# Block 0 by two half-size transposing DMAs, weight loads held back until the first loads have landed, and first projections of 256 columns

## The chip, the cores and the metric

The kernel runs on one core of a Trainium2 chip. Five engines work at once, each from an instruction queue of its own and in order: TensorE (PE in the profile, its weight loads shown as PEld), VectorE (DVE), ScalarE (ACT), GpSimd (POOL) and SyncE (SP). They wait for one another on semaphores. Transfers between the device memory and the on-chip memory are issued by SP and ACT and carried out by 16 DMA engines that both share. The metric is the device time of one launch in microseconds (us), as the median of several runs.

## The reference

The input `A_x` is one sequence of 2048 tokens with 512 features, in bfloat16. Two branches are computed from it and mixed by a gate:

```python
x = A_x                                            # (1, 2048, 512)
g = sigmoid((x * gate_w).sum(-1, keepdims=True))
# A: dilated local attention, 32 heads of 16, window 8, dilation 2
q, k, v = split(x @ wqkv)                          # wqkv (512, 1536)
logits[s, w] = q[s] . k[s - 2w] * 16**-0.5, masked where s - 2w < 0
a = (softmax(logits) weighted sum of v[s - 2w]) @ wo
# B: an MLP over the tokens, inner size 1792
h = layernorm(x)                                   # over the 512 features
b = transpose(gelu(h^T @ w1 + b1) @ w2 + b2)       # w1 (2048, 1792), w2 (1792, 2048)
return g * a + (1 - g) * b
```

All matrix products have bfloat16 operands and are summed in fp32.

## The kernel before

The kernel writes no instruction straight to an engine. It declares operations (`sch.add`, `sch.dma`, lines 89 to 124) with the names of the buffers that each reads and writes, an estimated duration, and extra dependencies: `deps` become real waits on semaphores, `after` only fixes an order. A planner (lines 126 to 232) then simulates the five queues with these estimates, and with 340 KB per us and 2 us of latency for transfers, and so settles the order of every queue before launch. On the chip each engine runs its list in that order and waits only for what an operation names.

What bears on the change is the beginning. The activations are wanted in two layouts: `X`, tokens on partitions (plain loads `ld_x`, four tiles of 128 tokens each), for the layer norm and the token MLP; and `XT`, features on partitions (transposing loads `ld_xt`), for the projections to q, k and v. `XT` comes in four blocks of 512 tokens, here called XT0 to XT3. The weights `wqkv` come as slices: q in two halves by the contraction (d0 and d1, then d2 and d3), here wq01 and wq23 of 256 KB each; all of k (wk, 512 KB); all of v (wv, 512 KB). The order of issue, lines 478 to 489, is

```python
ld_w(0, 0, 2, "act")   # wq01, the only load that ACT issues
ld_xt(0)               # all that follow are issued by SP, in this order
ld_w(0, 2, 2)          # wq23
ld_w(1, 0, 4)          # wk
ld_xt(1)
ld_x(0, 4); ld_x(4, 4); ld_xt(2); ld_xt(3); ld_x(8, 4); ld_x(12, 4); ld_w(2, 0, 4)
```

From the fifth load on, SP waits before an issue until the load five places earlier in the list `init_dmas` has landed (`throttle`, line 447).

While these loads are under way, PE multiplies zeros: nine matmuls of 512 columns (`warm1`, line 531). Then come the first projections (`pf_...`, lines 652 to 657): block 0 of q with d0 and d1 into four PSUM banks (8 matmuls of 512 columns), the same banks with d2 and d3 (8), and k of block 0 into the four other banks (16). ACT evicts each bank (`f_evq`). The list `seq_proj` follows: q and k of block 1, then of blocks 2 and 3, then v, and after that the gate (`emit_gz`), the first MLP product (line 848), the second (line 887), and the output projection (line 904). Between them lie short bursts of PE for the attention logits (`qkr`, line 693) that need products made by DVE (`qkm`, line 685); their place in PE's list is fixed by the planner. DVE begins with the layer norm's statistics (`ln1`, line 549) of the tiles that `ld_x(0, 4)` brings, and its order up to the softmax is written out by hand in `chain(...)`, lines 966 to 970.

Of the kernel before, what the change touches and what calls it, by code (L numbers as in the profile page):

```python
# [13 lines left out]
D = 512  # L14
# [321 lines left out]
def bass_gated_mix__sliding_local_dilated__mixer_token_mlp__prompt_kernel(nc, A_x, A_wqkv, A_wo, B_x, B_w1, B_b1, B_w2, B_b2, gate_w, out, dbg=None):  # L336
    with contextlib.ExitStack() as es:
        block = es.enter_context(nc.Block())
        view, pview, off, total = _views(nc, es)
        ps = es.enter_context(nc.psum_tensor("ps", [128, 8, 512], FP32))  # L340
        esem = {e: es.enter_context(nc.semaphore("sem_" + e)) for e in ("pool", "act", "dve", "pe")}
        sch = _Sched()

        x2d = A_x[0]
# [7 lines left out]
        XT = view("XT", BF16, [(S, 4), (1, S)])  # L352
# [68 lines left out]
        def sub(ap_, offs, dims):  # L421
            return bass.AP(ap_.tensor, ap_.offset + offs, [list(ap_.ap[0])] + [list(d) for d in dims])

        def psub(ap_, p0, np_, offs, dims):
            pst = ap_.ap[0][0]
            return bass.AP(ap_.tensor, ap_.offset + p0 * pst + offs, [[pst, np_]] + [list(d) for d in dims])

        A = sch.add
# [13 lines left out]
        def mk_dma(dst, src):  # L442
            return lambda e: e.dma_start(dst, src)

        init_dmas = []

        def throttle():
            return [init_dmas[-5]] if len(init_dmas) >= 5 else []

        def prev_dma():  # L450
            return [init_dmas[-1]] if init_dmas else []
# [9 lines left out]
        def ld_w(tn, d0, n, q="sp"):  # L461
            ds = sch.dsem("wqkv%d_%d" % (tn, d0))
            op = sch.dma(q, mk_dma(WQKV[:, d0:d0 + n, tn * D:(tn + 1) * D], wqkv_v[:, d0:d0 + n, tn * D:(tn + 1) * D]),
                         n * 128 * D * 2, ds, writes=["wqkv%d_%d" % (tn, dt) for dt in range(d0, d0 + n)],
                         deps=throttle() if q == "sp" and n == 4 else [], after=prev_dma() if q == "sp" else [],
                         issue=0.65 if n == 4 else 0.45, name="d_wp%d_%d" % (tn, d0))
            if q == "sp":
                init_dmas.append(op)
            return op

        def ld_xt(sb):
            ds = sch.dsem("xt%d" % sb)
            dst = XT[:, :, sb * 512:(sb + 1) * 512]
            op = sch.dma("sp", lambda e: e.dma_start_transpose(dst, x2d[sb * 512:(sb + 1) * 512, :]), 512 * D * 2, ds,
                         writes=["xt_%d" % t for t in range(4 * sb, 4 * sb + 4)], deps=throttle(), after=prev_dma(), name="d_xt%d" % sb)
            init_dmas.append(op)

        ld_w(0, 0, 2, "act")
        ld_xt(0)
        ld_w(0, 2, 2)  # L480
        ld_w(1, 0, 4)
        ld_xt(1)
        ld_x(0, 4)
        ld_x(4, 4)
        ld_xt(2)
        ld_xt(3)
        ld_x(8, 4)
# [4 lines left out]
                after=prev_dma(), name="d_gw", issue=0.3)  # L492
        sch.dma("sp", mk_dma(B1R, B_b1.rearrange("(t p) -> t p", p=128)), 4096, ds_b, writes=["b1r"], deps=throttle(),
                name="d_b1", issue=0.3)
        d_b2 = sch.dma("sp", mk_dma(B2R, B_b2.rearrange("(t p) -> t p", p=128)), 4096, ds_b, writes=["b2r"], deps=throttle(),
                       name="d_b2", issue=0.3)
# [16 lines left out]
        for g in range(4):  # L513
            d_wo = sch.dma("sp", mk_dma(psub(WO, 32 * g, 32, 0, [(D, 4), (1, D)]), wov[g]), 32 * 4 * D * 2, ds_wo,
                           writes=["wo%d" % g], deps=throttle(), name="d_wo%d" % g)
# [7 lines left out]
        def f_warm(n):  # L523
            def fn(e):
                ins = None
                for _ in range(n):
                    ins = e.matmul(ps[:, 7, :], lhsT=WARM[:, 0:128], rhs=WARM, start=True, stop=True)  # L527
                return ins
            return fn

        last_tx = A("pe", f_warm(9), 4.0, reads=["outs0"], writes=["lg7_0", "lg7_1"], name="warm1", prio=-100)

        ALLXT = ["xt_%d" % t for t in range(NST)]

# [11 lines left out]
        for hf in range(2):  # L546
            t0 = 8 * hf
            for t in range(t0, t0 + 8):
                A("dve", (lambda t_: (lambda e: e.bn_stats(out=ST6[:, t_, :], in_=X[:, t_, :])))(t), 0.59,  # L549
                  reads=["x%d" % t], writes=["st6_%d" % t], name="ln1_%d" % t, prio=0)  # L550
# [13 lines left out]
              reads=["zc%d" % hf], writes=["sd%d" % hf], name="ln_sqrt%d" % hf, prio=0)  # L564
            A("dve", (lambda t0_: (lambda e: e.reciprocal(out=cols(RSTD, t0_, 8), in_=cols(SD, t0_, 8))))(t0), 0.25,
              reads=["sd%d" % hf], writes=["rstd%d" % hf], name="ln_rstd%d" % hf, prio=0)
# [15 lines left out]
        last_main = [None]  # L582

        def main_bank():
            b = main_idx[0] % 4
            main_idx[0] += 1
            return b
# [40 lines left out]
            A("dve", lambda e: e.tensor_tensor(out=C2, in0=OMG, in1=B2C, op=ALU.mult), 0.15,  # L628
              reads=["omg", "b2c"], writes=["c2"], name="g_c2", prio=0)

        def f_proj(tn, dl, sb, bank, d0=0, d1=4):
            def fn(e):
                ins = None
                for dt in range(d0, d1):
                    lhsT = sub(WQKV, dt * 3 * D + tn * D + dl, [(4, 128)])
                    ins = e.matmul(ps[:, bank, :], lhsT=lhsT, rhs=XT[:, dt, sb * 512:(sb + 1) * 512],  # L636
                                   start=(dt == 0), stop=(dt == 3))
                return ins
            return fn

# [8 lines left out]
        tnames = ["q", "k", "v"]  # L649
        first = [(tn, dl) for tn in range(2) for dl in range(4)]  # L650
        fbn = [["acc%d" % b] for b in range(4)] + [["lg%d_0" % b, "lg%d_1" % b] for b in range(4, 8)]
        for (b0, d0, d1) in ((0, 0, 2), (0, 2, 4), (4, 0, 4)):
            for b in range(b0, b0 + 4):
                tn, dl = first[b]
                last_main[0] = A("pe", f_proj(tn, dl, 0, b, d0, d1), 0.216 * (d1 - d0),
                                 reads=ALLXT[0:4] + ["wqkv%d_%d" % (tn, dt) for dt in range(d0, d1)],
                                 writes=fbn[b], after=[last_main[0]], name="pf_%s%d_%d" % (tnames[tn], dl, d0))
        for b, (tn, dl) in enumerate(first):
            A("act", f_evq(tn, dl, 0, b), 0.52, reads=fbn[b] + (["k5pad"] if tn == 1 else []),
              writes=["%s5_%d_0" % (tnames[tn], dl)], name="ev_%s%d_0" % (tnames[tn], dl), prio=0)  # L660
# [7 lines left out]
        for (tn, dl, sb) in seq_proj:  # L668
            if (tn, dl, sb) == (2, 1, 0):
                emit_tb()  # L670
            xr = ALLXT[4 * sb:4 * sb + 4]
            bank = main_bank()
            last_main[0] = A("pe", f_proj(tn, dl, sb, bank), 0.866,
                             reads=xr + ["wqkv%d_%d" % (tn, dt) for dt in range(4)],
                             writes=["acc%d" % bank], after=[last_main[0]], name="pj_%s%d_%d" % (tnames[tn], dl, sb), prio=0)
            A("act", f_evq(tn, dl, sb, bank), 0.62, reads=["acc%d" % bank] + (["k5pad"] if tn == 1 else ["v5pad"] if tn == 2 else []),
              writes=["%s5_%d_%d" % (tnames[tn], dl, sb)], name="ev_%s%d_%d" % (tnames[tn], dl, sb), prio=0)
# [25 lines left out]
        for wh in range(2):  # L703
# [6 lines left out]
            for (dl, c0, nc_) in pieces:  # L710
# [3 lines left out]
                  reads=["q5_%d_%d" % (dl, sb) for sb in range(c0, c0 + nc_)] +  # L714
                        ["k5_%d_%d" % (dl, sb) for sb in range(max(c0 - 1, 0), c0 + nc_)] + ["k5pad"],
                  writes=wr, name="qkm_%d_%d_%d" % (wh, dl, c0), prio=0)
                if c0 + nc_ == 4 and dl % 2 == 1:
# [4 lines left out]
                    else:  # L722
                        for wl in range(4):
                            qop = A("pe", f_qkr(prs, (wl,)), 0.5, reads=rd, writes=["lg%d_0" % (4 + wl), "lg%d_1" % (4 + wl)],
                                    name="qkr_%d_%d_%d" % (wh, dl, wl), prio=-100 + wl, delay=BURST_DELAY)
                            A("act", (lambda wh_, wl_: (lambda e: e.activation(out=LGB[:, 4 * wh_ + wl_, :], in_=ps[:, 4 + wl_, :], func=AF.Copy)))(wh, wl),  # L726
                              0.55, reads=["lg%d_0" % (4 + wl), "lg%d_1" % (4 + wl)], writes=["lw%d" % (4 * wh + wl)],
                              name="lev_%d_%d" % (wh, wl), prio=0)
# [16 lines left out]
        def lw(hf):  # L745
            return ["lw%d" % w for w in range(4 * hf, 4 * hf + 4)]
# [6 lines left out]
        for hf in range(2):  # L753
# [3 lines left out]
              reads=["outs1"], writes=lw(hf), name="sm_sub%d" % hf, prio=0)  # L757
            if hf == 0:
                A("act", lambda e: e.activation(out=col(SD, 0), in_=col(ZC, 0), func=AF.Exp, scale=0.0), 1.5,
                  reads=["zc0"], writes=["sd0"], name="sm_pre")  # L760
            A("act", (lambda hf_: (lambda e: e.activation(out=ATT[:, 4 * hf_:4 * hf_ + 4, :], in_=LGB[:, 4 * hf_:4 * hf_ + 4, :],  # L761
                                                          func=AF.Exp)))(hf), 1.95,
              reads=lw(hf), writes=["att%d" % hf], name="sm_exp%d" % hf, prio=0)
# [10 lines left out]
        for hf in range(2):  # L774
# [3 lines left out]
              reads=["rs"], writes=["att%d" % hf], name="sm_nrm%d" % hf, prio=0)  # L778
# [3 lines left out]
        for c in range(4):  # L782
            for dh_hi in range(4):
                pst = V5.ap[0][0]
                src = bass.AP(V5.tensor, V5.offset + dh_hi * pst + 512 * c, [[4 * pst, 32], [KROW, 4], [1, VROW]])
                dst = psub(V3, 32 * c, 32, 4 * dh_hi * VSTR, [(VSTR, 4), (1, VROW)])
                v3_ops.append(sch.dma(V3Q, mk_dma(dst, src), 32 * 4 * VROW * 2, ds_v3, issue=(1.2 if V3Q == "pool" else 0.65),
                               reads=["v5_%d_%d" % (dl, sb) for dl in range(4) for sb in range(4)] + ["v5pad"],
                               writes=["v3_%d_%d" % (c, dh_hi)], deps=pb2_readers, name="d_v3_%d_%d" % (c, dh_hi)))
# [22 lines left out]
        for t in range(4):  # L812
            tb = []
            for wh in range(2):
# [3 lines left out]
                  writes=["pv%d_%d" % (buf, k_) for k_ in range(4)] + [qk_res, k_res, ["pb0_0", "pb0_1", "m4_0", "m4_1", "m2_0", "m2_1", "m1", "rs"]][buf],  # L818
                  name="avm_%d_%d" % (t, wh))
            b0, b1 = tb  # L820
            for (nm, o_, i_, n_, res) in (("ava", b0, b1, 4, None), ("avb", b0, b0, 2, 2), ("avc", b0, b0, 1, 1)):
# [4 lines left out]
                  writes=["pv%d_%d" % (o_, k_) for k_ in range(n_)], name="%s_%d" % (nm, t))  # L826
            if t < 3:
                ds_ot = sch.dsem("ot%d" % t)
                for c in range(4):
                    for g in range(4):  # L830
                        sch.dma("sp", mk_dma(psub(OT, 32 * g, 32, t * S + 512 * c, [(1, SC)]),
                                             psub(PV[b0], 32 * c, 32, g * SC, [(1, SC)])), 32 * SC * 2, ds_ot, issue=0.62,
                                reads=["pv%d_0" % b0], writes=["ot%d_%d_%d" % (t, c, g)], deps=v3_ops, name="d_ot%d_%d_%d" % (t, c, g))
            else:
                A("pe", f_ws(b0), 0.45, reads=["pv%d_0" % b0, "ident"], writes=LGA, name="ws_%d" % t, prio=-100, delay=BURST_DELAY)
                for c in range(4):
                    A("act", (lambda t_, c_: (lambda e: e.activation(out=OT[:, t_, 512 * c_:512 * c_ + 512], in_=ps[:, 4 + c_, :], func=AF.Copy)))(t, c),
                      0.55, reads=["lg%d_0" % (4 + c), "lg%d_1" % (4 + c)], writes=["ot%d_%d_%d" % (t, c, g) for g in range(4)], deps=v3_ops,
                      name="oev_%d_%d" % (t, c), prio=0)
# [13 lines left out]
        for ft in range(NFT):  # L853
            j = ft // 2
            bank = main_bank()
            p2 = A("pe", f_ph2(ft, bank, 0), 1.73, reads=["x%d" % t for t in range(8)] + ["w1s%d" % (j % 3)],
                   writes=["acc%d" % bank], after=[last_main[0]], name="ph2a_%d" % ft, prio=0)
            p2 = A("pe", f_ph2(ft, bank, 1), 1.73, reads=["x%d" % t for t in range(8, NST)] + ["w1s%d" % (j % 3)],
                   writes=["acc%d" % bank], after=[p2], name="ph2_%d" % ft, prio=0)
# [3 lines left out]
              reads=["acc%d" % bank, "b1c"], writes=["ut%d" % ft] + ALLXT,  # L863
              name="gel_%d" % ft, prio=0)
# [67 lines left out]
        for i in range(NST):  # L932
# [4 lines left out]
            elif i > 1:  # L937
                emit_ph3(i, 0)
            emit_ph3(i, 1)
            bank = p3bank[i]  # L940
            A("act", (lambda i_, bank_: (lambda e: e.activation(out=T1[:, i_, :], in_=ps[:, bank_, :], func=AF.Identity,  # L941
                                                               scale=col(OMG, i_), bias=col(C2, i_))))(i, bank), 0.8,
              reads=["acc%d" % bank, "omg", "c2"], writes=["t1_%d" % i, "lb0", "lb1"],
              name="t1_%d" % i, prio=0)
# [126 lines left out]
```

## Time and profile before

| | us |
|---|---|
| median of 3 runs (lowest, highest) | 172.16 (172.11, 172.23) |
| the profiled execution's own time | 172.07 |
| its span, first to last instruction | 170.3 |
| PE busy | 165.6 (97% of the span) |
| DVE busy | 142.4 (84%) |
| ACT busy | 76.2 (45%) |
| nine warm-up matmuls | 1.25 to 5.27 |
| first projection matmul starts | 5.77 |
| ACT's first eviction starts | 8.13 |
| DVE's first statistics start | 11.92 |
| last PE work ends | 167.33 |

The profile is of one execution. Times are counted from the start of its span. A busy PE is not PE at its peak: matmuls overlap, and the distance from one start to the next tells the rate. "To landing" is the time from the start of a DMA's issue until its data have arrived and its semaphore says so. The granted TensorE clock is shown as a share of full speed.

### The profile page before, as it was taken

The numbers are of one execution on the slowest core, as the hardware profiler recorded it, in microseconds if no ns is written. First come the engines' busy times: TensorE is split into PE (matmuls) and PEld (weight loads), VectorE is DVE, ScalarE is ACT, GpSimd is POOL, SyncE is SP. The second block draws the span as 40 slices with busy tenths as digits, with TensorE's granted clock in tenths as the row PEclk, the third lists the DMA queues.
The fourth block names the chain that finished last, engine by engine and source line by source line (L and its number), as shares of the span: only waits on it lengthen the run. The fifth ranks groups of instructions, "written<-read, shape, count | busy, mean of one in ns | idle before, by whom it ended". The sixth has DMA issues, their size and how long they took to land.

```text
span 170.3 us, 2192 instructions
## 1 busy us (share of the span) xinstructions
PE 165.6 (97%) x876; PEld 76.2 (45%) x876; DVE 142.4 (84%) x107; ACT 76.2 (45%) x117; POOL 0.9 (1%) x8
## 2 busy tenths in 40 slices
PE   7899999999999999999999999999999999999992
PEld 2355555544454444444444444444444444444440
DVE  1028999999999951899999999999999999916794
ACT  3087788898879716694211131131322313143000
POOL 2000000000000000000000000000000000000000
PEclk9999999999999999999999999999999999999999
DMA  5999999940002599999999302172877491001443
GB/s 144 312 301 235 309 316 229 271 108 4 0 0 73 93 158 113 263 204 290 294 290 290 82 15 54 49 214 72 216 202 211 109 257 51 8 0 62 153 159 123
DMA packets 50582, 26.97 MB, mean 158 GB/s; under 512 B 12168, under 2 KB 50568, under 8 KB 50572
## 3 DMA queue, kind: packets, MB, share of 16 engines
q1 hardware_dynamic: 50300, 26.57, 64.5%
q10 hardware_dynamic: 272, 0.26, 0.6%
q8 instruction: 7, 0.11, 0.3%
q14 instruction: 3, 0.02, 0.0%
HBM read 18.89 MB, written 2.11 MB: 123 GB/s over the span
## 4 chain that ended last, share of the span: by engine, by line
PE 95%; DMA 3%; DVE 0%; issue 0%
PE ps L848 29%; PE ps L887 28%; PE ps L636 25%; PE ps L904 8%; PE ps L693 4%; DMA arena<-in_A_x_dram 3%; PE ps L611 1%; DVE arena L916 0%; PE ps L802 0%; PE ps L594 0%; PE ps L596 0%; PE ps L595 0%
## 5 line engine op out<-in xcount | busy, mean ns | idle before, releaser
L848 PE MATMUL ps<-arena 128*128 128x512 bf16 x224 | 48.7, 379 | 0.0
L887 PE MATMUL ps<-arena 128*128 128x512 bf16 x224 | 48.7, 379 | 0.0
L636 PE MATMUL ps<-arena 128*128 128x512 bf16 x192 | 42.2, 379 | 0.5 <-DMA arena<-in_A_x_dram 0.5
L685 DVE TENSOR_TENSOR arena<-arena 128x4096 bf16<-128x4096 bf16 (+1 forms) x12 | 35.7, 2995 | 0.8 <-ACT arena L647 0.8
L795 DVE TENSOR_TENSOR arena<-arena 128x8192 bf16<-128x8192 bf16 x8 | 35.1, 4419 | 0.1
L848 PEld LDWEIGHTS ps<-arena 128*128 128x128 bf16 x224 | 21.7, 98 | 26.8 <-ACT arena L573 0.4
L887 PEld LDWEIGHTS ps<-arena 128*128 128x128 bf16 x224 | 21.8, 98 | 26.4 <-issue 0.2
L823 DVE TENSOR_TENSOR arena<-arena 128x8192 bf16<-128x8192 bf16 (+2 forms) x12 | 31.8, 2647 | 0.4
L636 PEld LDWEIGHTS ps<-arena 128*128 128x128 bf16 x192 | 21.4, 114 | 21.1 <-issue 1.4
L941 ACT ACTIVATE arena<-ps,arena 128x512 bf16<-128x512 f32 x16 | 12.5, 780 | 33.7 <-PE ps L887 33.7
L647 ACT ACTIVATE arena<-ps 128x512 bf16<-128x512 f32 x32 | 18.9, 596 | 5.4 <-PE ps L636 5.2
L861 ACT ACTIVATE arena<-ps,arena 128x512 bf16<-128x512 f32 x14 | 9.6, 688 | 24.5 <-PE ps L848 24.4
L549 DVE BATCH_NORM_STATS2 arena<-arena 128x6 f32<-128x512 bf16 x16 | 10.1, 681 | 10.2 <-DMA arena<-in_A_x_dram 10.2
L916 DVE SCALAR_TENSOR_TENSOR arena<-ps,arena 128x512 bf16<-128x512 f32 x16 | 11.8, 750 | 6.5 <-PE ps L904 4.5
L904 PE MATMUL ps<-arena 128*128 128x512 bf16 x64 | 14.0, 379 | 0.0
L644 ACT ACTIVATE arena<-ps 128x512 bf16<-128x512 f32 x16 | 9.0, 596 | 7.5 <-PE ps L636 7.5
L904 PEld LDWEIGHTS ps<-arena 128*128 128x128 bf16 x64 | 6.3, 98 | 7.6
L573 ACT ACTIVATE arena<-arena 128x512 bf16<-128x512 bf16 x12 | 9.3, 805 | 0.0
L743 DVE TENSOR_TENSOR arena<-arena 128x512 bf16<-128x512 bf16 (+3 forms) x10 | 7.1, 718 | 0.8 <-ACT arena L761 0.5
L693 PE MATMUL ps<-arena 128*32 128x512 bf16 x128 | 7.6, 380 | 0.0
L726 ACT ACTIVATE arena<-ps 128x512 bf16<-128x512 f32 x8 | 4.1, 602 | 3.3 <-PE ps L693 3.3
L527 PE MATMUL ps<-arena 128*128 128x512 bf16 x9 | 4.0, 631 | 1.2 <-DVE arena L521 1.2
(49 smaller groups left out, 36.4 us busy)
## 6 DMA issues: line engine op xcount, KB each, us to landing
arena<-in_B_w_dram SPq DMA_DIRECT2D x7, 1024.0 KB, 9.4
arena<-in_B_w_dram SPq DMA_DIRECT2D x8, 896.0 KB, 5.7
arena<-arena SPq DMA_DIRECT2D x16, 131.5 KB, 3.8
arena<-in_A_x_dram SPq DMA_DIRECT2D x4, 512.0 KB, 5.0
out_dram<-arena SPq DMA_DIRECT2D x16, 128.0 KB, 1.7
arena<-arena SPq DMA_DIRECT2D x48, 32.0 KB, 2.0
arena<-in_A_wqkv_dram SPq DMA_DIRECT2D x2, 512.0 KB, 5.7
arena<-in_A_wo_dram SPq DMA_DIRECT2D x4, 128.0 KB, 6.5
```

The source lines that it names most:

```text
L549: A("dve", (lambda t_: (lambda e: e.bn_stats(out=ST6[:, t_, :], in_=X[:, t_, :])))(t), 0.59, reads=["x%d" % t], writes=["st6_%d" % t], nam ...
L636: ins = e.matmul(ps[:, bank, :], lhsT=lhsT, rhs=XT[:, dt, sb * 512:(sb + 1) * 512], start=(dt == 0), stop=(dt == 3))
L647: return lambda e: e.activation(out=dst, in_=ps[:, bank, :], func=AF.Copy)
L685: return lambda e: e.tensor_tensor(out=PBL[buf][:, :, 512 * c0:512 * (c0 + nc_)], in0=in0, in1=in1, op=ALU.mult)
L693: ins = e.matmul(ps[32 * c:32 * c + 32, 4 + wl, :], lhsT=RP, rhs=PBL[buf][:, wl, c * 512:(c + 1) * 512], start=(dl == 0), stop=(dl == 3), ...
L795: return lambda e: e.tensor_tensor(out=PV[buf], in0=in0, in1=in1, op=ALU.mult)
L823: A("dve", (lambda o__, i__, n__, f__: (lambda e: e.tensor_tensor(out=PV[o__][:, 0:n__], in0=PV[o__][:, 0:n__], in1=PV[i__][:, f__:f__ + n ...
L848: ins = e.matmul(ps[:, bank, :], lhsT=W1W[:, slot, st, 128 * e_:128 * e_ + 128], rhs=X[:, st, :], start=(st == 0), stop=(st == NST - 1))
L887: ins = e.matmul(ps[:, bank, :], lhsT=W2S[slot][:, ft, 128 * e_:128 * e_ + 128], rhs=UT[:, ft, :], start=(ft == 0), stop=(ft == NFT - 1))
L904: ins = e.matmul(ps[:, WB(i), :], lhsT=OT[:, t, 128 * i:128 * i + 128], rhs=WO[:, t, :], start=(t == 0), stop=(t == 3))
L916: A("dve", (lambda i_: (lambda e: e.scalar_tensor_tensor(out=OUTS[:, i_ % 4, :], in0=ps[:, WB(i_), :], scalar=col(G, i_), in1=T1[:, i_, :] ...
L941: A("act", (lambda i_, bank_: (lambda e: e.activation(out=T1[:, i_, :], in_=ps[:, bank_, :], func=AF.Identity, scale=col(OMG, i_), bias=co ...
```

## The change

Block 0 of `XT` is loaded by two transposing DMAs of 256 tokens each (here XT0a and XT0b) on SP, in place of one of 512. The load wq23 moves from SP's queue to ACT's, behind a wait until wq01 has landed. The load wk stays on SP and gets a wait until XT0b has landed. Nine warm-up matmuls become six. The first pass of q over d0 and d1 is made in two sweeps over the four banks, columns 0 to 255 and then columns 256 to 511, and the first sweep names only XT0a's tiles; the second sweep's first matmul leaves out the start flag, since the first sweep's has already opened the bank. The planner is told the new durations.

```diff
+        def ld_xt0(h):
+            ds = sch.dsem("xt0_%d" % h)
+            dst = XT[:, :, h * 256:(h + 1) * 256]
+            op = sch.dma("sp", lambda e: e.dma_start_transpose(dst, x2d[h * 256:(h + 1) * 256, :]), 256 * D * 2, ds, issue=1.25,
+                         writes=["xt_%d" % t for t in range(2 * h, 2 * h + 2)], after=prev_dma(), name="d_xt0_%d" % h)
+            init_dmas.append(op)
+            return op
...
-        ld_w(0, 0, 2, "act")
-        ld_xt(0)
-        ld_w(0, 2, 2)
-        ld_w(1, 0, 4)
+        wq01 = ld_w(0, 0, 2, "act")
+        ld_xt0(0)
+        xt0b = ld_xt0(1)
+        wq23 = ld_w(0, 2, 2, "act")
+        wq23.deps.add(wq01)
+        wk = ld_w(1, 0, 4)
+        wk.deps.add(xt0b)
         ld_xt(1)
         ld_x(0, 4)
         ld_x(4, 4)
...
-        last_tx = A("pe", f_warm(9), 4.0, reads=["outs0"], writes=["lg7_0", "lg7_1"], name="warm1", prio=-100)
+        last_tx = A("pe", f_warm(6), 2.6, reads=["outs0"], writes=["lg7_0", "lg7_1"], name="warm1", prio=-100)
...
-        def f_proj(tn, dl, sb, bank, d0=0, d1=4):
+        def f_proj(tn, dl, sb, bank, d0=0, d1=4, s0=0, s1=512):
...
-                    ins = e.matmul(ps[:, bank, :], lhsT=lhsT, rhs=XT[:, dt, sb * 512:(sb + 1) * 512],
-                                   start=(dt == 0), stop=(dt == 3))
+                    ins = e.matmul(ps[:, bank, s0:s1], lhsT=lhsT, rhs=XT[:, dt, sb * 512 + s0:sb * 512 + s1],
+                                   start=(dt == 0 and s0 == 0), stop=(dt == 3))
...
-        for (b0, d0, d1) in ((0, 0, 2), (0, 2, 4), (4, 0, 4)):
+        for (b0, d0, d1, s0, s1) in ((0, 0, 2, 0, 256), (0, 0, 2, 256, 512), (0, 2, 4, 0, 512), (4, 0, 4, 0, 512)):
             for b in range(b0, b0 + 4):
                 tn, dl = first[b]
-                last_main[0] = A("pe", f_proj(tn, dl, 0, b, d0, d1), 0.216 * (d1 - d0),
-                                 reads=ALLXT[0:4] + ["wqkv%d_%d" % (tn, dt) for dt in range(d0, d1)],
-                                 writes=fbn[b], after=[last_main[0]], name="pf_%s%d_%d" % (tnames[tn], dl, d0))
+                last_main[0] = A("pe", f_proj(tn, dl, 0, b, d0, d1, s0, s1), 0.216 * (d1 - d0) * (s1 - s0) / 512,
+                                 reads=ALLXT[s0 // 128:s1 // 128] + ["wqkv%d_%d" % (tn, dt) for dt in range(d0, d1)],
+                                 writes=fbn[b], after=[last_main[0]], name="pf_%s%d_%d_%d" % (tnames[tn], dl, d0, s0))
```

## The prediction

> **What bounds the kernel now.** I began with the page's busy times and then followed the chain of work that ended last, in order of time.
>
> ```profile
> PE 165.6 (97%) x876; PEld 76.2 (45%) x876; DVE 142.4 (84%) x107; ACT 76.2 (45%) x117; POOL 0.9 (1%) x8
> ```
> ```profile
> 0.80 4.83 DMA arena<-in_A_x_dram
> 5.63 0.14 issue
> 5.77 28.65 PE ps L636 x132
> 34.42 1.84 PE ps L693 x32
> ...
> 153.50 13.83 PE ps L904 x64
> ```
>
> After XT0 lands (0.80 + 4.83 = 5.63) and a wake of 0.14, PE works from 5.77 to 167.33 with no gap. So the only time to win or lose is ahead of PE's stream or in a hole torn into it. The stream must be followed slice by slice: 16 q matmuls need XT0 and wq01, then wq23, then 16 k matmuls need wk. The timeline of PE gives the rate:
>
> ```profile
> 4.64 0.63 PE L527 MATMUL ps<-arena 128*128 128x512 bf16 x1
> ...
> 5.77 0.81 PE L636 MATMUL ps<-arena 128*128 128x512 bf16 x3 [0.50 <-DMA arena<-in_A_x_dram]
> ```
>
> Three projections in 0.81 us, one lasting 0.38, are (0.81 - 0.38) / 2 = 0.215 from start to start, call it 0.216. So k begins at 5.77 + 16 x 0.216 = 9.23: the date that the change must beat. The nine warm-up matmuls stand 0.427 apart (1.25 to 4.64 in eight steps of 0.424).
>
> Next, the timeline of the issuing queues, and the DMA view in narrow windows around each issue, for the time to landing (last column):
>
> ```profile
> 0.80 0.41 ACTq L443 DMA_DIRECT2D arena<-in_A_wqkv_dram  x1
> 0.80 1.43 SPq L474 DMA_TRANSPOSE arena<-in_A_x_dram  x1
> ...
> 2.29 1.72 SPq L443 DMA_DIRECT2D arena<-in_A_wqkv_dram  x2
> 4.05 3.69 SPq L474 DMA_TRANSPOSE arena<-in_A_x_dram  x1
> ```
> ```profile
> arena<-in_A_wqkv_dram ACTq DMA_DIRECT2D x1, 256.0 KB, 2.8
> arena<-in_A_x_dram SPq DMA_TRANSPOSE x1, 4.8
> ```
> ```profile
> arena<-in_A_wqkv_dram SPq DMA_DIRECT2D x1, 512.0 KB, 4.4
> ```
> ```profile
> arena<-in_A_x_dram SPq DMA_DIRECT2D x1, 512.0 KB, 4.1
> ```
>
> wq01 lands at 0.80 + 2.8 = 3.6. wq23, issued at 2.29, lands 4.1 later at 6.4. wk is issued at 3.50 (the first of the pair takes 1.21) and lands at 3.50 + 4.4 = 7.9, with 9.23 - 7.9 = 1.33 to spare. The last row is x0, issued at 7.79 and landed at 11.9.
>
> Last, the table by windows (length, POOL busy, granted clock, DMA share, GB/s) shows what the pipe does:
>
> ```profile
> 2.25:2.50 0.25, 0.00 (x0) 1.00 0.39 111
> 2.75:3.00 0.25, 0.00 (x0) 1.00 1.10 361
> 4.25:4.50 0.25, 0.00 (x0) 1.00 1.28 291
> 6.00:6.50 0.50, 0.00 (x0) 1.00 1.10 344
> ```
>
> It fills only around 2.5. The stretch at 291 GB/s is XT0 alone, in packets under 512 B; its first packets move after 2.6, its last near 4.95, 0.7 before it lands. Plain loads run at 344 to 361.
>
> **The change, part by part.** I sum on the profiled execution: 172.07, of which 170.3 is the span and 1.77 lies around it; the median is 0.09 higher. As PE has no gap behind 9.23, the time moves by what the start of k moves, if nothing later tears.
>
> *XT0 in halves.* SP issues two transposes. The issue of a half costs between half of 1.43 and all of it. At 0.72 the data begin 0.7 sooner than now and XT0b lands at best at 5.63 - 0.70 = 4.93. At 1.43 each, the second issue ends near 3.72, its data begin 0.47 later (2.70 against an issue end of 2.23 in XT0), take 1.0 and need 0.7 to land: 5.9. I take 5.63: the bytes are the same and wq01 moves beside them as now. XT0a's packets are done half-way, near 3.95, and land at 4.65; PE starts at 4.79, 0.98 sooner than now. That gain is real, but only the next slices can keep it.
>
> *q over d0 and d1 in 256 columns.* 16 matmuls in place of 8, with 8 more weight loads. A half should take 0.108; a weight load here takes 0.113. Between 16 x 0.108 = 1.73 (loads all hidden) and 16 x 0.221 = 3.54 (none hidden) I take 0.12 each, since the loads hide behind matmuls today. First sweep: 4.79 to 5.75; XT0b is there at 5.77; second sweep to 6.73. At the upper end the sweeps end at 8.33 and q at 10.06, later than wk below.
>
> *wq23 on ACT behind wq01.* Issued at 3.6 + 0.14 = 3.74. With wq01's own 2.8 it lands at 6.54, with today's 4.1 at 7.84; I take 2.8, as the pipe ahead holds only XT0's rest. Behind the wait on ACT stand the table load (1.28, today at 1.24) and the first eviction (8.13 today); nobody asks for either before 7. Its former issue on SP (1.21) goes. The eight matmuls over d2 and d3 run from 6.73 to 8.46, or to 9.71 at the late end (7.84 + 0.14 + 1.73).
>
> *wk waits for XT0b.* This is the price. Issue moves from 3.50 to 5.63 + 0.14 = 5.77, and nothing is queued ahead of it any more. Its time to landing in an empty pipe is shown by no row of its size. wq01's 2.8 plus another 256 KB at 350 GB/s (0.75) makes 3.55; x0's 4.1, with the tail of XT1 ahead, is the nearest in size; its own 4.4 had XT0's rest and wq23 ahead. I take 3.8, between the first two, and keep 3.5 and 4.4. It lands at 9.57 and k starts at 9.71: 0.48 later than now, with PE idle from 8.46 to 9.71.
>
> The Trainium skill ("DMA: Bandwidth & Descriptors", Rules for kernel authors) speaks against this part: issue a DMA early and wait late, so that its fixed cost overlaps. The trace agrees in that wq01 needed 2.8 us for 256 KB. By the page's fit of 2.0 us plus bytes / 436 GB/s, measured on another issuing path, wk would take 3.2, an estimate, and k would start at 9.11, 0.12 sooner than now; the 4.1 of x0 does not bear that out.
>
> *All else behind wk on SP.* XT1 follows wk. Its long issue ended 0.16 before wk landed (7.74 against 7.9), so now near 9.4, and it lands 2 us later at 11.4; PE wants it at 9.71 + 3.46 = 13.17. XT2 and XT3, which land at 15.4 and 17.4 today, slip by some 1.7 to 17.1 and 19.1 and are wanted at 20.1 and 21.0. wv, w1 and wo have over 5 us. x0 lands at 9.47 + 4.1 = 13.57, and the statistics end 2.47 later at 16.04:
>
> ```profile
> 11.92 2.47 DVE L549 BATCH_NORM_STATS2 arena<-arena 128x6 f32<-128x512 bf16 x4 [10.23 <-DMA arena<-in_A_x_dram]
> ```
> ```profile
> 15.23 4.49 DVE L685 TENSOR_TENSOR arena<-arena 128x4096 bf16<-128x4096 bf16 x2 [0.84 <-ACT arena L647]
> ```
> ```profile
> 30.84 2.27 DVE L685 TENSOR_TENSOR arena<-arena 128x4096 bf16<-128x4096 bf16 x1
> ```
>
> DVE's products then begin 0.81 late, PE being 0.48 late. The first burst of logits wants them at 34.42 and has them at 33.11: a slack of 1.31, which takes the difference of 0.33. The issues wait five places back as before; the two changed partners have landed long since. POOL's queue has no part in it. The planner's new durations could move a burst; I count nothing, as its later order hangs on hand-written chains.
>
> *Six warm-up matmuls.* They end near 1.25 + 6 x 0.427 = 3.81, so PE idles some 1.0 before 4.79 where it idled 0.5. Taken by itself nothing is lost, if the rate of 0.216 is there at 4.79.
>
> Sum: 172.16 + 0.48 = 172.64; I say 172.6.
>
> **Rivals.**
>
> *Cold start.* PE ran at 0.427 until 4.64 and at 0.216 from 5.77, so the rate rose 3.4 to 4.5 after the first matmul, while the granted clock read 1.00 throughout. With 2.6 us of warm-up and a hole, it may rise only that long after 4.79. Then the sweeps take 16 x 0.213 = 3.41, to 8.20, and q ends at 9.93 (+0.70); if it rises only at 4.79 + 4.5 = 9.3, some 2.6 matmuls over d2 and d3 are slow too, and q ends at 10.47 (+1.24). Time 172.9 to 173.4. For it speaks the shortened warm-up; against it that the hole is under a third of the stretch. The Trainium skill ("TensorE: Matmul & The Clock Gate", Part 1) has it that full rate comes after about 3.4 us of sustained activity; the trace's 3.4 to 4.5 agrees.
>
> *wk comes sooner, and the gain is kept (the faster side).* XT0b at 4.93 and wk in 3.55 give 4.93 + 0.14 + 3.55 + 0.14 = 8.76, 0.47 sooner: 171.7. It decides from k starting before 8.89, which needs landing of XT0b plus wk's time below 8.61; I have 9.43. For it speaks the pipe at 111 GB/s near 2.3, room for an earlier half; against it x0's 4.1.
>
> *The change does nothing to the end.* XT0b comes midway, at 5.28, and wk takes 3.55 to 3.8: k at 9.11 to 9.36, time 172.04 to 172.29. The wait costs what the earlier landing and the empty pipe give, and PE's early start is waited away. For it speaks that the forecast is only 0.35 from it; against it, as for the faster side, that two values must both come out lower than the nearest row.
>
> **How the numbers follow.** A 0.2% difference, 0.34 us, is about what a measurement of this kernel can tell from no change. The forecast (k later by 0.13 to 1.0, wk last) has 0.55, 0.10 of it within that bound; the cold start 0.17, all slower; the faster rival 0.15, 0.12 of it beyond the bound; no effect 0.13, 0.03 of it faster. So slower 0.62, same 0.10 + 0.03 + 0.10 = 0.23, faster 0.15. The range runs from 171.75, just inside the faster end, to 173.3, which takes in XT0b at 5.9 with wk at 4.2 and most of the cold start. The forecast alone has 172.29 to 173.16.
>
> **What would show it.** Right: XT0a lands near 4.65 and matmuls start near 4.8; wk is issued near 5.8 and lands near 9.6; PE has one hole of about 1.2 ahead of k, and none later. Wrong: a first sweep at 0.21 per half (cold start); no hole before k (wk early, or q slow); a hole at the first burst of logits near 34 (x0 too late for DVE); XT0b landing after 6, if a transpose waits for the one before.

## The result and the profile after

| | before | after |
|---|---|---|
| median of 6 runs (lowest, highest), us | 172.15 (172.02, 172.24) | 173.27 (172.93, 173.66) |
| span of the profiled execution | 170.3 | 171.7 |
| first projection matmul | 5.77 | 4.91 |
| first k matmul | 9.22 | 10.52 |
| last PE work ends | 167.33 | 168.66 |

The changed kernel is slower: ratio 1.0062, 95% interval 1.0048 to 1.0075. It also spreads more, 0.73 us between its runs against 0.22. Here and below the ratios leave out runs more than 1.5% above the fastest of the same kernel, so they need not equal the ratio of the two medians.

The chain that ended last, in order of time, for the kernel after (start, length, what):

```profile
0.80 3.98 DMA arena<-in_A_x_dram
4.78 0.14 issue
4.91 30.83 PE ps L647 x140
35.74 1.84 PE ps L704 x32
```

XT0a lands at 4.78 and PE begins at 4.91, 0.86 sooner. But the first burst of logits starts at 35.74, 1.32 later than before (34.42). So 2.2 us went between 4.91 and 35.74, and the rest of the span only carries this along: the last PE work is 1.33 late. The timeline of the issuing queues, and of PE in narrow windows, kernel after, shows where; the last line is the weight load for k:

```profile
0.80 3.23 ACTq L443 DMA_DIRECT2D arena<-in_A_wqkv_dram  x2
0.80 2.77 SPq L474 DMA_TRANSPOSE arena<-in_A_x_dram  x2
...
6.52 0.44 SPq L443 DMA_DIRECT2D arena<-in_A_wqkv_dram  x1
7.01 3.26 SPq L482 DMA_TRANSPOSE arena<-in_A_x_dram  x1
```
```profile
4.91 0.80 PE L647 MATMUL ps<-arena 128*128 128x256 bf16 x3 [0.92 <-DMA arena<-in_A_x_dram]
...
8.28 0.97 PE L647 MATMUL ps<-arena 128*128 128x512 bf16 x2
...
10.16 0.76 PE L647 MATMUL ps<-arena 128*128 128x512 bf16 x2
```
```profile
10.51 1.44 PEld L647 LDWEIGHTS ps<-arena 128*128 128x128 bf16 x8 [0.44 <-DMA arena<-in_A_wqkv_dram]
```

Of the matmuls of 256 columns, the second starts at 5.08 and the sixteenth at 8.06: one every 0.213 us, which at 512 columns would be one every 0.43, the rate of the warm-up. The six warm-up matmuls stand 0.427 apart as well, so nothing shows PE at the full rate before this. The slow rate lasts until the start at 8.71, and from 9.09 on the starts stand 0.216 apart. The last q matmul starts at 10.16, so that PE could begin k at 10.38; the first of k starts at 10.52.

The DMA view of the kernel after, around the issue of XT0b, wq23 and wk (time to landing in the last column):

```profile
arena<-in_A_x_dram SPq DMA_TRANSPOSE x1, 4.3
```
```profile
arena<-in_A_wqkv_dram ACTq DMA_DIRECT2D x1, 256.0 KB, 3.6
```
```profile
arena<-in_A_wqkv_dram SPq DMA_DIRECT2D x1, 512.0 KB, 3.9
```

XT0b, issued at 2.23, lands at 6.50; SP then issues wk at 6.52, and it lands at 10.47 (the expectation below has 10.41). So two things end within 0.1 us of each other, a slow q (10.38) and a late wk (10.47). In this execution wk is the later: the weight load for k, at 10.51, has waited for it. What the time would be without the one or the other takes experiments.

### The profile page after: what moved, and what is told of

The parts are those of the page before. It is cut to its first block, busy times and chain, and to the rows that moved or that the text cites. A ratio compares the mean times of both kernels' runs of the same rounds, so it can differ in the third digit from the quotient of the medians.

```text
span 171.7 us, 2203 instructions
## 1 busy us (share of the span) xinstructions
PE 166.5 (97%) x881; PEld 77.1 (45%) x881; DVE 142.2 (83%) x107; ACT 76.2 (44%) x117; POOL 0.9 (1%) x8
## 4 chain that ended last, share of the span: by engine, by line
PE 95%; DMA 2%; DVE 0%; issue 0%
PE ps L859 28%; PE ps L898 28%; PE ps L647 26%; PE ps L915 8%; PE ps L704 4%; DMA arena<-in_A_x_dram 2%; PE ps L622 1%; DVE arena L927 0%; PE ps L813 0%; PE ps L605 0%; PE ps L607 0%; PE ps L606 0%
## 5 line engine op out<-in xcount | busy, mean ns | idle before, releaser
L859 PE MATMUL ps<-arena 128*128 128x512 bf16 x224 | 48.7, 379 | 0.0
L898 PE MATMUL ps<-arena 128*128 128x512 bf16 x224 | 48.7, 379 | 0.0
L647 PE MATMUL ps<-arena 128*128 128x512 bf16 (+1 forms) x200 | 44.4, 385 | 0.9 <-DMA arena<-in_A_x_dram 0.9
L859 PEld LDWEIGHTS ps<-arena 128*128 128x128 bf16 x224 | 21.7, 98 | 26.9 <-ACT arena L584 0.4
L898 PEld LDWEIGHTS ps<-arena 128*128 128x128 bf16 x224 | 21.8, 98 | 26.4 <-issue 0.2
L647 PEld LDWEIGHTS ps<-arena 128*128 128x128 bf16 x200 | 22.8, 117 | 22.4 <-issue 2.3
L915 PE MATMUL ps<-arena 128*128 128x512 bf16 x64 | 14.0, 379 | 0.0
L915 PEld LDWEIGHTS ps<-arena 128*128 128x128 bf16 x64 | 6.3, 98 | 7.5
L704 PEld LDWEIGHTS ps<-arena 128*32 128x32 bf16 x128 | 3.1, 97 | 4.1 <-issue 0.8
```

What stands on the lines that cost most here:

```text
L647: ins = e.matmul(ps[:, bank, s0:s1], lhsT=lhsT, rhs=XT[:, dt, sb * 512 + s0:sb * 512 + s1], start=(dt == 0 and s0 == 0), stop=(dt == 3))
L704: ins = e.matmul(ps[32 * c:32 * c + 32, 4 + wl, :], lhsT=RP, rhs=PBL[buf][:, wl, c * 512:(c + 1) * 512], start=(dl == 0), stop=(dl == 3), ...
L859: ins = e.matmul(ps[:, bank, :], lhsT=W1W[:, slot, st, 128 * e_:128 * e_ + 128], rhs=X[:, st, :], start=(st == 0), stop=(st == NST - 1))
L898: ins = e.matmul(ps[:, bank, :], lhsT=W2S[slot][:, ft, 128 * e_:128 * e_ + 128], rhs=UT[:, ft, :], start=(ft == 0), stop=(ft == NFT - 1))
L915: ins = e.matmul(ps[:, WB(i), :], lhsT=OT[:, t, 128 * i:128 * i + 128], rhs=WO[:, t, :], start=(t == 0), stop=(t == 3))
```

## The experiments

Two theories: W, the wait puts wk's landing too late; C, the shortened warm-up makes q slow. Each kernel was compared with the kernel before on the same chip. The median of the kernel before was 172.16 for the first four experiments, 172.30 for the six warm-ups alone, the halves alone, wq23's move alone and the version with d0 first, and 172.29 for the other three. One execution of each kernel was traced, and what is read from a trace is of that one. In the diffs long lines are cut off at the right, and `...` stands for lines left out.

**Nine warm-ups again** (in the changed kernel).

```diff
-        last_tx = A("pe", f_warm(6), 2.6,
+        last_tx = A("pe", f_warm(9), 4.0,
```

> The changed kernel with nine warm-up matmuls again. In the changed kernel q ends at 10.38 and wk lands at 10.41, so two causes meet. Theory W (the wait for XT0b alone sets the start of k): matmuls at full rate from about 5.1, q done near 9.2, a hole of 1.3 us on PE, k at 10.5 as before the edit; time 173.1 to 173.3, with less spread from run to run than the 0.73 us of the changed kernel. Theory C (the cold start alone sets it): k starts near 9.2, time 172.1.

Measured: 173.54 (173.11 to 174.06), ratio 1.0076 (1.0057 to 1.0094). Its timeline:

```profile
5.08 1.04 PE L647 MATMUL ps<-arena 128*128 128x256 bf16 x8 [0.23 <-DMA arena<-in_A_x_dram]
6.34 0.44 SPq L443 DMA_DIRECT2D arena<-in_A_wqkv_dram  x1
6.37 2.79 PE L647 MATMUL ps<-arena 128*128 128x256 bf16 x16 [0.26 <-DMA arena<-in_A_x_dram]
...
10.38 3.65 PE L647 MATMUL ps<-arena 128*128 128x512 bf16 x16 [1.21 <-DMA arena<-in_A_wqkv_dram]
```

The cold start is gone (eight pieces in 1.04, q done at 9.16) and nothing is gained: PE waits 1.21 for wk and k starts at 10.38. This is W, though the median is 0.2 above what W foresaw (the traced execution, 173.24, lies within it). The smaller spread that W foresaw did not come (0.95 us), so the spread is there without the cold start too.

**Without wk's wait, six warm-ups** (in the changed kernel).

```diff
-        wk.deps.add(xt0b)
```

> The changed kernel with wk's wait for XT0b taken out; six warm-up matmuls as in the change. Theory W: wk is issued near 3.6 and lands before 8.6, and the time falls by 1.0 or more, to 172.2 or less. Theory C: q is as slow as before and ends near 10.4, k starts there; time 173.0 to 173.2. If both causes are each enough, this and the run with nine warm-ups stay slow, each for its own reason.

Measured: 173.09 (172.76 to 175.57), ratio 1.0038 (1.0023 to 1.0053). The traced execution, 174.14, is one of the slower. The cold start lies in it as expected of C, but it isn't what ends last:

```profile
9.27 0.61 PE L647 MATMUL ps<-arena 128*128 128x512 bf16 x1 [0.67 <-DMA arena<-in_A_wqkv_dram]
```

The cold sweeps end at 8.6 and PE then waits until 9.27 for wq23, which I had not expected: it takes 5.6 us here against 3.6 in the changed kernel.

**Nine warm-ups and no wait** (in the changed kernel).

```diff
-        last_tx = A("pe", f_warm(6), 2.6,
+        last_tx = A("pe", f_warm(9), 4.0,
...
-        wk.deps.add(xt0b)
```

> The changed kernel with nine warm-up matmuls and without wk's wait. If the wait and the cold start are together the whole loss: q at full rate, second sweep behind XT0b at 6.5, wq23 at 7.3, q done near 9.2, k at 9.2; time 172.0 to 172.3, that of the kernel before. If the two half transposes or ACT's later wq23 cost something by themselves, it stays above 172.4.

Measured: 173.59 (173.15 to 173.75), ratio 1.0074 (1.0058 to 1.0090). The expectation missed: with both suspects removed the loss stays. Timeline and DMA view:

```profile
3.64 0.58 SPq L443 DMA_DIRECT2D arena<-in_A_wqkv_dram  x1
...
6.81 1.06 PE L647 MATMUL ps<-arena 128*128 128x256 bf16 x8 [0.75 <-DMA arena<-in_A_x_dram]
8.99 5.37 PE L647 MATMUL ps<-arena 128*128 128x512 bf16 x24 [1.12 <-DMA arena<-in_A_wqkv_dram]
```
```profile
arena<-in_A_wqkv_dram ACTq DMA_DIRECT2D x1, 256.0 KB, 5.3
```

PE waits for XT0b (0.75) and for wq23 (1.12); the eight matmuls over d2 and d3 run from 8.99, and k starts at 10.75. With the wait the same load took 3.4 to 3.6. So the wait on wk had protected wq23, which now stands on the other queue and is issued when SP's queue already holds XT0b and wk. Two more parts of the change are under suspicion: the halves and the move to ACT.

**The two waits alone, on the kernel before.**

```diff
-        ld_w(0, 0, 2, "act")
-        ld_xt(0)
-        ld_w(0, 2, 2)
-        ld_w(1, 0, 4)
+        wq01 = ld_w(0, 0, 2, "act")
+        xt0 = ld_xt(0)
+        wq23 = ld_w(0, 2, 2, "act")
+        wq23.deps.add(wq01)
+        wk = ld_w(1, 0, 4)
+        wk.deps.add(xt0)
```

> The kernel before (one transpose of 512 rows, nine warm-ups, matmuls of 512 columns) with the two waits alone: wq23 on ACT behind wq01, wk behind XT0. Theory W: XT0 lands at 5.63, wk is issued at 5.8 and lands 3.9 later at 9.7, k starts at 9.8 instead of 9.23; time 172.6 to 172.8. If the late landing of XT0b in the changed kernel (6.4) comes from the waits and not from the halves, XT0 lands late here too and the time is 173 or more. Theory C: no cold start here, so 172.2.

Measured: 172.68 (172.51 to 173.45), ratio 1.0032 (1.0020 to 1.0044), as W has it:

```profile
5.64 0.43 SPq L443 DMA_DIRECT2D arena<-in_A_wqkv_dram  x1
...
9.62 4.72 PE L639 MATMUL ps<-arena 128*128 128x512 bf16 x21 [0.25 <-DMA arena<-in_A_wqkv_dram]
```

wk is issued at 5.64 and k starts at 9.62. Against the run with nine warm-ups, which has the same waits and the same warm-up, the halves with their sweeps are the one difference, and there wk is issued at 6.34 and k starts at 10.38. So under the waits the halves cost 0.76 (0.86 by the medians). The table by windows (length, POOL busy, granted clock, DMA share, GB/s) shows the transposes, first with one transpose of 512 rows (this run), then with two of 256 (nine warm-ups):

```profile
3.80:4.20 0.40, 0.00 (x0) 1.00 1.27 290
4.20:4.60 0.40, 0.00 (x0) 1.00 1.27 288
4.60:5.00 0.40, 0.00 (x0) 1.00 1.22 238
```
```profile
3.80:4.20 0.40, 0.00 (x0) 1.00 1.03 229
4.20:4.60 0.40, 0.00 (x0) 1.00 0.89 195
4.60:5.00 0.40, 0.00 (x0) 1.00 1.16 235
5.00:5.40 0.40, 0.00 (x0) 1.00 1.17 176
```

One transpose holds 290 GB/s and is nearly done by 5.0. Two of them fall to 195 to 235, and the last packets of the second move after 5.4. An obvious suspect is wq23, which ACT has issued in the meantime. The DMA view of the run with nine warm-ups, from 4.2 to 5.0, clears it: SP's queue (q1) is the only one that moves packets there.

```profile
DMA packets 673, 0.17 MB, mean 215 GB/s; under 512 B 673, under 2 KB 673, under 8 KB 673
q1 hardware_dynamic: 673, 0.17, 102.6%
```

So the second transpose is slow without another queue beside it; why, no run here shows.

**Six warm-ups alone, on the kernel before.**

```diff
-        last_tx = A("pe", f_warm(9), 4.0,
+        last_tx = A("pe", f_warm(6), 2.6,
```

> The kernel before with six warm-up matmuls and nothing else changed. Cold start: PE idles from 4.0 to 5.77 and the projections then start 0.427 us apart until 3.8 to 4.2 us after 5.77 (in the changed kernel the rate rose 3.8 to 4.2 after its first projection); 9 or 10 slow matmuls lose 0.21 each, k starts about 2 us late; time 173.9 to 174.3. If the warm-up does not matter here: 172.2.

Measured: 173.93, but the ten runs fall in two groups: 172.02, 172.21 and 172.37, and seven from 173.69 to 175.31. Ratio 1.0051 (1.0007 to 1.0095). The profiled one is of the second group:

```profile
6.08 1.44 PE L636 MATMUL ps<-arena 128*128 128x512 bf16 x3 [2.08 <-DMA arena<-in_A_x_dram]
```

Three matmuls in 1.44, the last of them 0.6: 0.43 apart. They stay so until 10.3, 4.2 us after 6.08, as C had it. Three runs of ten show no such loss in their time; as only one run was traced, that the cold start is what parts the groups is likely and not shown. The two groups lie some 1.8 us apart. In the traced execution of the changed kernel the cold start costs nothing, since wk lands after q.

**The halves alone** (wq23 and wk back on SP behind XT0b, no waits, nine warm-ups).

```diff
-        wq23 = ld_w(0, 2, 2, "act")
-        wq23.deps.add(wq01)
-        wk = ld_w(1, 0, 4)
-        wk.deps.add(xt0b)
+        ld_w(0, 2, 2)
+        ld_w(1, 0, 4)
```

> The two half transposes and the first sweep in 256 columns alone: nine warm-ups, wq23 and wk on SP directly behind XT0b as in the kernel before, no added wait. If the halves cost something by themselves (each takes 1.37 us to issue, so wq23's issue moves from 2.3 to 3.6 and XT0b lands at 6.2 to 6.4 instead of 5.63): wq23 lands near 7.7, q ends near 9.5, wk lands near 9.3, time 172.4 to 172.7. If the loss lies in the added waits and in ACT's queue alone: q ends at 9.2 or before, 172.2 or less.

Measured: 172.44 (172.00 to 172.79), ratio 1.0001 (0.9978 to 1.0024): the median is where the first case had it, but the interval doesn't tell it from no change. The trace is clearer. The first projection starts at 5.86, no sooner than with one transpose, since XT0a lands only at 5.7; the sweeps and the pass over d2 and d3 end at 9.57, where k starts. So halving alone did not bring XT0a early in this trace. It isn't the wait on wk that does, either: without it XT0a landed at 4.89 in both runs above. What these have and this one lacks is wq23 on ACT behind wq01; that this is the reason is not shown.

**wq23's move alone** (on ACT behind wq01, all else as before).

```diff
-        ld_w(0, 2, 2)
+        wq23 = ld_w(0, 2, 2, "act")
+        wq23.deps.add(wq01)
```

> The kernel before with one edit: wq23 on ACT behind wq01, wk free on SP behind XT0 (one transpose of 512 rows, nine warm-ups). If wq23 is delayed by sharing the pipe with wk, which now stands ahead of it in time (as in the run without the wait, where it took 5.3 us): it lands near 8.5 to 9, the matmuls over d2 and d3 wait from 7.5, k starts 1.0 to 1.5 late, time 173.1 to 173.6. If it took 5.3 only because of the halves: 172.2.

Measured: 172.88 (172.80 to 174.27), ratio 1.0031 (1.0003 to 1.0058), and

```profile
arena<-in_A_wqkv_dram ACTq DMA_DIRECT2D x1, 256.0 KB, 4.5
```

Issued at 3.6, it lands at 8.1; the matmuls over d2 and d3 start at 8.16 and not at 7.5. k starts at 9.92, 0.70 late. The direction is the expected one, at 0.6 instead of 1.0 to 1.5. With the two waits, where nothing follows XT0 on SP, the same load took 2.9.

**wk behind XT0a** (in the changed kernel, with nine warm-ups): a third date for wk's issue.

```diff
-        wk.deps.add(xt0b)
+        wk.deps.add(xt0a)
```

> The changed kernel with nine warm-ups, and wk waiting for XT0a instead of XT0b. The three dates of wk's issue are then 3.6 (no wait), about 4.9 (here) and 6.3 (wait for XT0b). If the wait sets the start of k: wk is issued at 4.9 and lands 4.0 to 4.4 later, at 8.9 to 9.3; q ends near 9.1; k starts near 9.4, time 172.3 to 172.5. If instead wk only takes the pipe from XT0b and wq23 as it did without the wait: wq23 lands after 8.5 and k starts after 10.2, time 173.1 or more.

Measured: 172.70 (172.52 to 173.57), ratio 1.0023 (0.9997 to 1.0050). Timeline, then PE's waits (us in total, times, longest):

```profile
5.10 0.43 SPq L443 DMA_DIRECT2D arena<-in_A_wqkv_dram  x1
```
```profile
PE ps L647 <- DMA arena<-in_A_wqkv_dram: 0.8, 1, 0.8
PE ps L647 <- DMA arena<-in_A_x_dram: 0.2, 1, 0.2
```

wk is issued at 5.10, lands 4.7 later, and k starts at 9.83; wq23 keeps its 3.4. The expectation missed: the time lies between its two cases, and wk took longer than the 4.0 to 4.4 foreseen. So the dates of issue 3.64, 5.10 and 6.34 give k at 10.75, 9.83 and 10.38: too early squeezes wq23, too late wk itself. None of the three reaches 9.22.

**Halved by features** (in the changed kernel: each transpose 512 rows by 256 features, first pass in 512 columns, both waits, nine warm-ups).

```diff
-            dst = XT[:, :, h * 256:(h + 1) * 256]
+            dst = XT[:, 2 * h:2 * h + 2, 0:512]
...
-            op = sch.dma("sp", lambda e: e.dma_start_transpose(dst, x2d[h * 256:(h + 1) * 256, :]),
+            op = sch.dma("sp", lambda e: e.dma_start_transpose(dst, x2d[0:512, h * 256:(h + 1) * 256]),
...
```

> The changed kernel with nine warm-ups and both waits, but block 0 halved by features (each transpose 512 rows by 256 features, so the first pass needs only the first one and runs in 512 columns). If two transposes one behind the other are slow whatever their shape: the second lands at 6.2 to 6.4 as with 256 rows, wk lands near 10.3, k starts near 10.4, time 173.1 to 173.6. If the 256-row shape is at fault: it lands near 5.7, k starts near 9.7, time 172.6 to 172.8, as with one transpose and the same waits.

Measured: 173.23 (173.07 to 173.56), ratio 1.0052 (1.0027 to 1.0077). wk is issued behind the second transpose at

```profile
6.25 0.43 SPq L443 DMA_DIRECT2D arena<-in_A_wqkv_dram  x1
```

and k starts at 10.29, as the first case had it. The shape isn't at fault; two transposes in the place of one are.

**A version meant to gain: only d0 of q ahead of XT0** (on the kernel before).

```diff
-        ld_w(0, 0, 2, "act")
+        ld_w(0, 0, 1, "act")
         ld_xt(0)
+        ld_w(0, 1, 1)
         ld_w(0, 2, 2)
...
-        for (b0, d0, d1) in ((0, 0, 2), (0, 2, 4), (4, 0, 4)):
+        for (b0, d0, d1) in ((0, 0, 1), (0, 1, 2), (0, 2, 4), (4, 0, 4)):
```

> A version meant to gain: the kernel before, but ACT loads only the d0 slice of q (128 KB) ahead, d1 follows XT0 on SP, then wq23 and wk as before; the first pass over the four banks is split into d0 and d1. If the 256 KB of wq01 hold back the first packets of XT0 (they share the pipe until 3.1): XT0 lands 0.2 to 0.4 sooner, d1 lands before 6.3, k starts as much sooner; time 171.8 to 172.0. If XT0's landing does not hang on wq01, or d1 comes too late: 172.2 or more.

Measured: 172.05 (171.52 to 172.45), ratio 0.9962 (0.9927 to 0.9998). Four of the 35 runs of the kernel before beside it lie at 174.3 to 174.5 and widen the interval; by medians (172.05 against 172.30) the gain is 0.25, between the two cases. XT0 lands at 5.1, half a microsecond sooner, with fewer bytes ahead of it:

```profile
arena<-in_A_wqkv_dram ACTq DMA_DIRECT2D x1, 128.0 KB, 2.3
arena<-in_A_x_dram SPq DMA_TRANSPOSE x1, 4.3
```
```profile
arena<-in_A_wqkv_dram SPq DMA_DIRECT2D x1, 128.0 KB, 4.4
```

But d1 lands at 6.7 and PE, idle from 6.25, waits 0.53 for it. By the medians this kernel is faster than the other two, by little; its traced execution (172.22, above the median) doesn't show the gain, for k starts at 9.39 there, 0.17 later than before.

**The same with d1 on ACT behind d0.**

```diff
-        ld_w(0, 0, 1, "act")
+        wq0 = ld_w(0, 0, 1, "act")
         ld_xt(0)
-        ld_w(0, 1, 1)
+        wq1 = ld_w(0, 1, 1, "act")
+        wq1.deps.add(wq0)
```

> The version with the d0 slice first, but with d1 on ACT behind d0's landing instead of on SP behind XT0 (there it took 4.4 us, landed at 6.7 and left PE waiting from 6.1). If ACT's queue brings d1 sooner: issued at 3.25, landed by 6.2 to 6.5, k starts 0.2 to 0.5 sooner than there; time 171.6 to 171.9. If the pipe behind XT0 is what d1 waits for: it lands at 6.7 or later again and the time is 172.0 or more.

Measured: 172.84 (172.47 to 173.20), ratio 1.0022 (0.9998 to 1.0045). The second case came: d1 takes 4.7 for 128 KB and lands at 7.7, later than from SP's queue, which had issued it 0.7 sooner and took 4.4. k starts at 10.37. Once more a load that ACT issues after SP's queue has filled comes late.

## Why the prediction was right, and where it was off

The direction and the place held: the time moved by what the start of k moved (1.30 in the trace, 1.12 by the medians), and no hole appears behind it. All runs bear this out: in the thirteen traced executions, the two kernels and eleven experiments, k starts anywhere from 9.22 to 11.58, and the execution's own time less the start of k is always 162.83 to 162.89. wk's wait is a part of the price, as forecast, but the smaller part: k starts 0.40 later by the waits alone and 0.76 later again by the halves. The time forecast, 172.6, was 0.7 too low. The measured 173.27 lies just inside the range, which ended at 173.3, and above the forecast's own 172.29 to 173.16; the room at that end had been left for the cold start, which did not set the time, and for an XT0b at 5.9 with a wk of 4.2, where XT0b came later and wk sooner. That the range held is partly luck. Of the prediction's own signs of being wrong three came: a first sweep at 0.213 per half, no hole worth the name ahead of k (0.14), and XT0b landing after 6.

- *XT0a and PE's start.* 4.65 and 4.79 forecast, 4.78 and 4.91 measured.
- *XT0b's landing.* This is the step that failed: "I take 5.63: the bytes are the same and wq01 moves beside them as now", with 5.9 as the upper end. It landed at 6.50 (6.32 with nine warm-ups). The issue of a half costs 1.37, nearly that of a whole (1.43). The prediction's upper sum had this; with the issue of the second half ending at 3.57 it gives 3.57 + 0.47 + 1.0 + 0.7 = 5.74. The rest is a second transpose that moves its packets at 195 to 235 GB/s where one alone holds 290, which the prediction did not have. The term was 0.87 too small and the landing lay outside its bounds; the run with the waits alone, where one transpose lands at 5.6 and k starts at 9.62, is the forecast's own sum (9.71) with its own XT0.
- *wk's time to landing.* 3.8 taken, 3.9 measured, and 3.9 again with the waits alone. The Trainium skill's advice on issuing early ("DMA: Bandwidth & Descriptors", Rules for kernel authors) held: the two waits by themselves cost 0.52. That page's fit, made on another issuing path, gives 3.2 as an estimate; wk took 3.94 at the least in these runs.
- *wq23.* Landing 6.54 taken, 7.84 kept as the late end; it was 3.64 + 3.61 = 7.25.
- *256 columns.* 0.12 a piece taken, 0.108 measured at the full rate (nine warm-ups), where the weight loads hide; 0.213 in the changed kernel, by the cold start.
- *The cold start.* I gave it 0.17 and it came about in the profiled execution, with q's end at 10.38 between the two dates worked out (9.93 and 10.47). But it isn't what made the kernel slow: with nine warm-ups k starts at 10.38 and the time is no lower. Part by part, the start of k goes from 9.22 to 9.62 by the waits and to 10.38 by the halves. The last 0.14, to 10.52, is not the cold start's: in both executions k starts 0.05 after wk has landed, and wk was issued 0.18 later in the changed kernel because XT0b landed 0.18 later.
- *The rival of no effect and the faster one* needed XT0b at 5.28 or sooner. It was 1.2 us from that.
- *x0 and DVE.* x0 was to land at 13.57 and landed at 10.32 + 4.1 = 14.4, for the same reason as wk; DVE's first products started at 16.85, 1.62 late, against 1.32 on PE, and the slack of 1.31 at the first burst took the difference.

What stays open: why the changed kernel spreads over 0.73 us and the one with nine warm-ups over 0.95, why XT0b lands at different dates from kernel to kernel (5.93 to 6.82), and why the second transpose is slow in the DMA engines.

## What to carry to other kernels

A load that is held back so that an earlier one may land sooner must be costed from its own deadline: here wk had 1.33 us to spare, and the wait and its fresh start cost more than that. A first transfer cut in two helps only if the second half isn't dearer than half a whole; look at what one issue costs and at two such transfers in a row before cutting. When two causes end within 0.1 us of each other, removing either shows nothing, and removing both can uncover a third: change the parts one at a time on the kernel before as well. Look also for the one start that the time hangs on: here the time less the start of k was the same within 0.06 us in thirteen executions, and only what stands ahead of that start had to be explained.

## What the runs showed of the hardware

- The rate of the matmuls rises at very different dates. The dates here are estimates, from the one distance between two starts that lies between the slow 0.427 us and the fast 0.216 (0.213 and 0.108 at 256 columns). All first matmuls start at 1.25. With nine warm-ups the rise comes near 3.9 (wq23's move), 4.3 (nine warm-ups on the changed kernel), between 4.6 and 5.8 (before), near 5.8 (feature halves), 6.4 (halves alone), and after 6.4 (d1 on ACT): 2.7 to over 5.1 us after the first matmul, a wider stretch than the 3.4 to 4.5 that the prediction read from one trace. With six it comes near 9.0 (after), 9.9 (without wk's wait) and 10.3 (six on the kernel before). The granted clock reads 1.00 all the while. The Trainium skill ("TensorE: Matmul & The Clock Gate", Part 1) says that the activity window runs freely and so the number of slow matmuls varies from run to run; the dates here and the two groups of runs with six warm-ups agree.
- A transpose of 256 rows costs 1.37 us to issue, one of 512 rows 1.43; with the same two waits the second of two halves, of either shape, lands at 6.23 to 6.50, a whole at 5.62.
- A load issued by ACT while SP's queue is full of others comes late: 256 KB took 2.9 to 3.6 with wk held back from that queue, 4.5 to 5.6 with it there; 128 KB took 4.7, against 4.4 from SP. The Trainium skill ("DMA: Bandwidth & Descriptors", Issuing engines are not separate DMA queues) says that all queues interleave on the same engines, so that a second one only saves time of issue. These runs agree in that wq23 never landed sooner from ACT (6.49 at best) than from SP in the kernel before (6.39); with wk on SP's queue it landed 1.7 later (8.12).
